# Low parts of the first layer's operands during attention: from DVE (five of seven) to POOL (all seven)

## The chip, the cores and the metric

One core of a Trainium2 chip runs the whole program. The metric is the device time of one launch in microseconds. The engines are TensorE (PE; its weight loads are listed as PEld), VectorE (DVE), ScalarE (ACT), GpSimd (POOL) and SyncE (SP, which only issues DMAs here). Each engine works through its own instructions in program order; between engines, semaphores keep the order of reads and writes.

## What is computed

An attention with a bias that a small network makes from positions, then two layers of experts that are all used, with their weights. Cut to what matters:

```python
# q, k, v: (2, 8, 576, 64)
scores = scale * q @ k.T + bias          # bias from |i - j|, through 32 hidden units
attn = softmax(scores)                   # by rows
x = (attn @ v)                           # -> (1152, 512)
# layer 1: 4 experts, given weights p        layer 2: 8 experts, weights P from a gate (Sinkhorn, 8 rounds)
for e in range(E):
    h = np.maximum(x @ w1[e], 0.0)       # 512 -> 1024
    out += p[:, e:e + 1] * (h @ w2[e])   # 1024 -> 512
```

## The kernel before

All matrix products of the expert layers are made from split numbers: an operand is written as a high part (a copy rounded to the matmul's format, made by ACT, L103) and a low part (the value less its high part, a subtraction, L104), and three products of parts are added. The first product of an expert (x @ w1) also uses a fast scheme with seven products in place of eight, so x is kept as seven operands: A11, A12, A22 are blocks of x, and S1 to S4 are sums and differences of blocks. `pieces(1, 0)` makes these operands for the first five token tiles ("chunk 0") of layer 1, out of the rows that attention has finished. Each tile of x10A and x10S in the profile is one of them.

The chunk has 5 pieces of 64 columns. A piece has three parts, and after the last there is one more flush:

- part1 first calls `flush()`, which issues the low parts that are pending from the part before. Then the engine `eng` makes t1 = a21 + a22 (L117), a21 = a11 - a21 in place (L118) and t2 = t1 - a11 (L119). Then `split` has ACT make the high parts of A12, A11 and S1 at once, and puts their low parts on the list of pending ones, in this order.
- part2 flushes (the low parts of A12, A11, S1), then `eng` makes a12 = a12 - t2 in place (L126); S2 and A22 are split.
- part3 flushes (S2, A22), then splits S3 (from a21) and S4 (from a12). Their low parts are issued by the flush of the next part1.

The parts are called with two engines, `eng` = DVE (`ve`) and `other` = POOL (`gp`): A11 and A22 have their low part made by `other`, the five others by `eng`.

They are worked off one by one in the attention's loop over the units k = 0 to 38. A unit is one pair of heads, one batch entry and one tile of 128 rows; there are 36. The order of work is written out by hand. In iteration k the engines get, in this order:

- DVE: emit_x(k-4) (L514: the output rows of unit k-4, from PSUM), then the scores of unit k are made on PE (L388), after the transposes (L443) of the tail of unit k-2, and its spread reciprocals, into the same PSUM tile. Then DVE's two maxima of unit k (L406, one for each head, which also write the scores to SBUF), then the reciprocal for unit k-1 (L429), after which POOL spreads it over 128 columns (L431).
- ACT: the first exponential of unit k (L419), the copy of the tail of unit k-2 (L488), its share of the copies of the transposed scores (L488), in the first half also two copies of the bias (L362), the second exponential of unit k. DVE makes the other copy (L486) or, while the bias is still being made, the hidden units (L319).
- POOL: L425 for unit k, which adds a small number to the two sums of the exponentials and so waits for the second exponential of unit k.
- PE: the product with V of unit k-3 (L504).
- DVE: the split of the queries for a later unit (L256, L257), in some iterations.
- one part of the pieces, in k = 16 to 18 and 23 to 35. So part1 stands in 16, 23, 26, 29 and 32, part2 in 17, 24, 27, 30 and 33, part3 in 18, 25, 28, 31 and 34, the last flush in 35.
- from k = 28, one step of the split of the first weights: POOL low parts of 128x512 (L170), with their high parts on ACT (L169), and differences on DVE (L166).

When the loop is over, the first layer begins (L751). The lines of the pieces and their calls:

Of the kernel before, what the change touches and what calls it, by code (L numbers as in the profile page):

```python
# [48 lines left out]
def attn_moe_moe(ctx: ExitStack, tc: tile.TileContext, pack, keep, rel, qT, kT, vT, w, out):  # L49
    nc = tc.nc  # L50
    pe, ve, sc, gp, sy = nc.tensor, nc.vector, nc.scalar, nc.gpsimd, nc.sync

    def pool(name, space=None, bufs=1, stack=ctx, side=None):
        kw = {} if space is None else {"space": space}
        if side is not None:
            kw["side"] = side
        if space is not DRAM:
            kw["reuse_waits"] = "tile"
        return stack.enter_context(tc.tile_pool(name=name, bufs=bufs, **kw))
# [25 lines left out]
    def col_tile(k):  # L85
        return row_tile(k).rearrange("p (k c) -> p k c", k=4)
# [4 lines left out]
    def pieces(layer, c):  # L91

        n = CHUNKS[c][1]
        for i in XA:
            X[layer, c, i] = xpools[c].tile([128, 2, 2, n], F32R, tag=f"x{c}{i}", name=f"x{layer}{c}{i}")


        pending = []

        def split(i, src, o, w, lo):  # L100
            x = X[layer, c, i]
            hi = x[:, 0, :, o:o + w]
            sc.activation(out=hi, in_=src, func=AF.Copy)  # L103
            pending.append(lambda: lo.tensor_tensor(out=x[:, 1, :, o:o + w], in0=src, in1=hi.bitcast(F32), op=ALU.subtract))  # L104

        def flush(eng=None, other=None):
            while pending:
                pending.pop(0)()

        def piece(k1, c1, k2, c2, w, o):  # L110
            h1, h2 = col_tile(k1)[:, :, c1:c1 + w], col_tile(k2)[:, :, c2:c2 + w]
            a11, a12, a21, a22 = h1[:, 0:2], h1[:, 2:4], h2[:, 0:2], h2[:, 2:4]
            t1, t2 = (g1.tile([128, 2, 128], F32, tag=f"t{i}", name=f"t{i}_{layer}{k1}")[:, :, 0:w] for i in range(2))

            def part1(eng, other):
                flush()
                eng.tensor_tensor(out=t1, in0=a21, in1=a22, op=ALU.add)  # L117
                eng.tensor_tensor(out=a21, in0=a11, in1=a21, op=ALU.subtract)  # L118
                eng.tensor_tensor(out=t2, in0=t1, in1=a11, op=ALU.subtract)  # L119
                split("A12", a12, o, w, eng)  # L120
                split("A11", a11, o, w, other)
                split("S1", t1, o, w, eng)

            def part2(eng, other):
                flush()
                eng.tensor_tensor(out=a12, in0=a12, in1=t2, op=ALU.subtract)  # L126
                split("S2", t2, o, w, eng)
                split("A22", a22, o, w, other)

            def part3(eng, other):  # L130
                flush()
                split("S3", a21, o, w, eng)
                split("S4", a12, o, w, eng)

            return [part1, part2, part3]

        return [part for x in CHUNKS[c][2] for part in piece(*x)] + [flush]
# [46 lines left out]
    def attention(moe):  # L184
# [232 lines left out]
        def emit_exp(u, h):  # L417
            s = sm[u][:, S * h:S * h + S]
            sc.activation(  # L419
                out=s, in_=s, func=AF.Exp, scale=-1.0,  # L420
                bias=stat[u][:, h:h + 1], accum_out=stat[u][:, 2 + h:3 + h],
            )
# [4 lines left out]
        def emit_recip2(u):  # L427
            st = stat.pop(u)
            ve.reciprocal(st[:, 6:8], st[:, 4:6])  # L429
            spread[u] = atb.tile([128, 128], F32, tag="spread", name=f"spread{u}", bufs=2)  # L430
            gp.tensor_copy(  # L431
                spread[u].rearrange("p (h d) -> p h d", h=2), st[:, 6:8].unsqueeze(2).to_broadcast([128, 2, D])
            )
# [78 lines left out]
        def emit_x(u):  # L512
            t, p, b = units[u]
            ve.tensor_tensor(  # L514
                out=rows[t][:, b, 128 * p:128 * p + 128],
                in0=po[t, p][:, 128 * b:128 * b + 128], in1=rc.pop(u), op=ALU.mult,
            )
# [6 lines left out]
        def busy(n):  # L524
            for _ in range(n):
                pe.matmul(out=po_all[:, 0, 0:128], lhsT=ones, rhs=ones, start=True, stop=True)  # L526
# [73 lines left out]
        ti, work, first_split = 0, [], None  # L600
        for k in range(U + 3):
            first = False
            if made == NGR and not apart:
                st_tq.close()
                tq, apart = pool("tr", PSUM, stack=st_tq, side="right"), True
            if k == FOUR:
                st_sc.close()
                ps, four = pool("ps4", PSUM, stack=st_sc, side="left"), True
            if k < U:
                t, p, b = units[k]  # L610
                first = b == 0
                if first:
                    ti = tps_.index((t, p))
                if k >= 4:
                    emit_x(k - 4)
                emit_S(k)
                if k < 3:
                    busy(6)
                emit_max(k)

                if (t == 4 or b == 1) and ti in follows:
                    wanted.append(follows[ti])
                while wanted and NEED[tps_[wanted[0]][0]] <= made:
                    load_bias(wanted.pop(0))
                if k > 0:
                    emit_recip2(k - 1)
                if first and ti + 4 < len(tps_):
                    load_q(*tps_[ti + 4])
                if k < 2:
                    load_k(*kq[k + 6])  # L630
                if k < 8 and k % 2 == 0:
                    load_v(k // 2)
            elif k == U:
                emit_recip2(k - 1)
                emit_x(k - 4)
                st_sc.close()
                st_a.close()
                moe.open1()
                first_layer = moe.L1(0)
                for fn in first_layer[0:3]:  # L640
                    fn()
            if k < U:
                emit_exp(k, 0)
                if k >= 2:
                    emit_evac(k - 2, 2, sc)
            if k >= 2 and k - 2 < U:
                emit_T(k - 2)
                one = made < NGR
                emit_evac(k - 2, 3 if one else 0, sc)
                if k >= U:  # L650
                    emit_evac(k - 2, 2, sc)
            if k < FOUR:
                emit_exp(k, 1)
            groups(1)
            if FOUR <= k < U:
                emit_exp(k, 1)
            if k >= 2 and k - 2 < U:
                if not one:
                    emit_evac(k - 2, 1, ve)
            hids(2)  # L660
            if k < U:
                emit_recip(k)
            hids(2)
            if k >= 3 and k - 3 < U:
                emit_P(k - 3)
                if k >= U:
                    emit_x(k - 3)

            if first:
                if ti + 2 < len(tps_) and tps_[ti + 2][0] < 4:  # L670
                    prep_q(*tps_[ti + 2])
            prep_lows()
            if k < 4:
                prep_k(*kq[k + 4], sc)
            if k == 8:
                gp.memset(wgr, 0.0)
                gp.tensor_copy(wgr[:, :, 0:E2], kept[:, K_WG:K_WG + 32].rearrange("p (k e) -> p k e", e=E2))
                ve.tensor_reduce(out=psm, in_=dp, axis=mybir.AxisListType.X, op=ALU.add)
                ve.tensor_scalar(psm, psm, 1e-9, None, op0=ALU.add)
                ve.reciprocal(psm, psm)  # L680
                ve.tensor_tensor(out=p1, in0=dp, in1=psm.unsqueeze(2).to_broadcast([128, NTT, E1]), op=ALU.mult)
            if k == 15:
                work = pieces(1, 0)
            if work and (15 < k < 19 or 22 < k):
                work.pop(0)(ve, gp)
            if k == 24:
                load_raw(0)
            if 28 <= k < U:
                if first_split is None:
                    first_split = moe.prefetch(-1, gp)  # L690
                if first_split:
                    first_split.pop(0)()
            if k == U:
                second_split = moe.prefetch(-1, ve)
                for fn in second_split[0:4] + first_layer[3:5]:
                    fn()
            if k == U + 1:
                for fn in first_layer[5:] + second_split[4:]:
                    fn()
# [409 lines left out]
```

## Time and profile before

| | us |
|---|---|
| median of the runs | 1336.52 (1336.31 to 1337.37) |
| profiled execution | 1338.04, of it a span of 1335.9 from the first to the last instruction |
| PE busy in the span | 1310.9 (98%) |
| DVE busy | 784.5 (59%) |
| ACT busy | 518.0 (39%) |
| POOL busy | 434.0 (32%) |

Shares of busy time are means over the attention (to about 171 us) and the two layers behind it, which have different limits. Times below are microseconds from the start of the span. In a timeline the time in square brackets is how long the engine was idle just before, and what ended that; a line without brackets began with no idle time worth a note. An instruction's duration includes its tail, which overlaps the next one of the same engine.

### The profile page before, as it was taken

What the parts mean: (1) busy time and instruction counts of PE and PEld (TensorE: products, weight loads), DVE (VectorE), ACT (ScalarE), POOL (GpSimd) and SP (SyncE); (2) the same over time, 40 slices, a digit from 0 to 9 for tenths busy, and PEclk for the clock granted to TensorE, in tenths of its full rate; (3) what the DMA queues carried; (4) which work ended last, traced back from release to release, by engine and by line L of the source; (5) the groups of instructions that cost most, each with busy time, mean ns of one, the idle gap of its engine ahead of it and who ended that gap; (6) DMA issues with size and microseconds to landing.
All of it is one profiled execution on the core that took longest, in us unless ns stands there. A gap on an engine that the chain in (4) does not pass through costs nothing.

```text
span 1335.9 us, 23119 instructions
## 1 busy us (share of the span) xinstructions
PE 1310.9 (98%) x9105; PEld 1147.5 (86%) x9105; DVE 784.5 (59%) x1766; ACT 518.0 (39%) x1208; POOL 434.0 (32%) x457
## 2 busy tenths in 40 slices
PE   7999899999999999999999999999999999999998
PEld 4777788898888898888888898998988988988987
DVE  7899967454553644864864644644735635645633
ACT  5899853441331422543342421422422413313311
POOL 5443432350440530450530620621612603504400
PEclk8999999999999999999999999999999999999999
DMA  7876421020110110020110210210201200201010
GB/s 228 225 221 165 136 66 43 32 95 0 64 65 0 64 64 1 32 96 1 64 64 1 65 62 1 95 32 1 95 32 33 95 0 33 95 1 63 33 40 32
DMA packets 34316, 84.71 MB, mean 63 GB/s; under 512 B 8864, under 2 KB 9120, under 8 KB 34208
## 3 DMA queue, kind: packets, MB, share of 16 engines
q1 hardware_dynamic: 31184, 75.60, 17.9%
q0 software_dynamic: 2880, 7.34, 2.0%
q8 instruction: 71, 1.16, 0.4%
q14 instruction: 37, 0.30, 0.1%
q10 hardware_dynamic: 144, 0.29, 0.1%
HBM read 69.97 MB, written 13.25 MB: 62 GB/s over the span
## 4 chain that ended last, share of the span: by engine, by line
PE 88%; DVE 5%; ACT 3%; DMA 2%; issue 1%; POOL 1%; SPq 0%; ACTq 0%; POOLq 0%; DVEq 0%
PE y L830 43%; PE B L751 16%; PE C L751 11%; PE A L751 11%; PE po L504 2%; PE sc L388 2%; PE bps L333 1%; DMA bd<-bsts 1%; DVE s L406 1%; ACT s L419 1%; ACT bsts L362 1%; DMA rawb<-in_w 1%; ACT at L488 1%; PE po L526 1%; PE tp L467 1%
## 5 line engine op out<-in xcount | busy, mean ns | idle before, releaser
L830 PE MATMUL y<-gb,h 128*128 128x512 f32 x2592 | 713.5, 395 | 0.0
L830 PEld LDWEIGHTS y<-gb,h 128*128 128x128 f32 x2592 | 450.7, 188 | 56.6 <-issue 0.4
L170 POOL TENSOR_TENSOR gb<-rawb,gb 128x512 fp32r<-128x512 f32 x94 | 122.9, 1322 | 630.3 <-ACT gb L169 625.8
L759 DVE TENSOR_TENSOR u<-B,s 128x320 f32<-128x320 f32 (+1 forms) x192 | 87.9, 458 | 334.7 <-PE B L751 334.7
L762 ACT ACTIVATE h<-c 128x320 fp32r<-128x320 f32 (+1 forms) x288 | 120.0, 439 | 366.3 <-DVE c L759 365.1
L765 DVE SCALAR_TENSOR_TENSOR h<-c,h 128x320 fp32r<-128x320 f32 (+1 forms) x288 | 180.1, 642 | 50.6 <-ACT h L762 45.6
L170 POOL TENSOR_TENSOR ga<-rawa,ga 128x512 fp32r<-128x512 f32 x94 | 127.6, 1376 | 3.3 <-ACT ga L169 3.2
L170 POOL TENSOR_TENSOR ga<-wt,ga 128x512 fp32r<-128x512 f32 x94 | 107.5, 1163 | 25.4 <-ACT ga L169 14.5
L759 DVE TENSOR_TENSOR c<-C,u 128x320 f32<-128x320 f32 (+1 forms) x192 | 87.2, 454 | 39.7 <-PE C L751 36.1
L773 ACT ACTIVATE s<-A 128x320 f32<-128x320 f32 (+1 forms) x96 | 39.5, 411 | 162.3 <-PE A L751 162.3
L169 ACT ACTIVATE gb<-rawb 128x512 fp32r<-128x512 f32 x96 | 60.0, 626 | 88.4 <-DMA rawb<-in_w 88.4
L762 ACT ACTIVATE h<-A 128x320 fp32r<-128x320 f32 (+1 forms) x96 | 39.0, 406 | 137.2 <-PE A L751 137.1
L759 DVE TENSOR_TENSOR c<-B,s 128x320 f32<-128x320 f32 (+1 forms) x96 | 43.9, 457 | 74.4 <-PE B L751 73.2
L751 PE MATMUL B<-x20S,ga 128*128 128x320 f32 x384 | 66.6, 309 | 0.0
L751 PE MATMUL C<-x20S,ga 128*128 128x320 f32 x384 | 66.6, 309 | 0.0
L751 PE MATMUL A<-x20A,ga 128*128 128x320 f32 x384 | 66.6, 309 | 0.0
L751 PEld LDWEIGHTS A<-x20A,ga 128*128 128x128 f32 x384 | 61.5, 188 | 5.7
L751 PEld LDWEIGHTS C<-x20S,ga 128*128 128x128 f32 x384 | 61.3, 188 | 5.7
L751 PEld LDWEIGHTS B<-x20S,ga 128*128 128x128 f32 x384 | 61.3, 188 | 5.6
L419 ACT ACTIVATE s<-s,stat 128x576 f32<-128x576 f32 x72 | 55.4, 770 | 11.3 <-DVE stat L406 9.6
L751 PEld LDWEIGHTS C<-x21S,ga 128*128 128x128 f32 x384 | 54.4, 188 | 6.3 <-DVE c L759 0.7
L751 PEld LDWEIGHTS A<-x21A,ga 128*128 128x128 f32 x384 | 54.5, 189 | 5.6
(194 smaller groups left out, 1880.7 us busy)
## 6 DMA issues: line engine op xcount, KB each, us to landing
rawa<-in_w SPq DMA_DIRECT2D x48, 512.0 KB, 4.0
rawb<-in_w SPq DMA_DIRECT2D x48, 512.0 KB, 4.9
bd<-bsts SPq DMA_DIRECT2D x36, 295.5 KB, 4.4
bt<-bd SPq DMA_DIRECT2D x13, 512.0 KB, 4.6
qr<-in_qT POOLq DMA_DIRECT2D x40, 64.0 KB, 3.7
kr<-in_kT POOLq DMA_DIRECT2D x16, 144.0 KB, 4.0
V<-in_vT POOLq DMA_DIRECT2D x4, 512.0 KB, 5.1
out<-rows SPq DMA_DIRECT2D x8, 256.0 KB, 2.1
```

The costliest lines, as they stand in the source:

```text
L169: sc.activation(out=z(0), in_=src, func=AF.Copy)
L170: lo.tensor_tensor(out=z(1), in0=src, in1=z(0).bitcast(F32), op=ALU.subtract)
L333: pe.matmul(out=o[32 * q:32 * q + 32, j, 0:n], lhsT=w2n, rhs=hid[g, q][:, n * j:n * j + n], start=True, stop=True,)
L388: pe.matmul(out=o[h][c:c + n, j, 0:288], lhsT=a[d, 128 * bb + c:128 * bb + c + n], rhs=m[d, 288 * j:288 * j + 288], start=t == 4 or i == 0 ...
L419: sc.activation(out=s, in_=s, func=AF.Exp, scale=-1.0, bias=stat[u][:, h:h + 1], accum_out=stat[u][:, 2 + h:3 + h],)
L504: pe.matmul(out=o[64 * h:64 * h + 64, c0:c0 + n], lhsT=V[p][:, j, col:col + D], rhs=rhs, start=j == 0, stop=j == 4,)
L751: pe.matmul(out=ban[o], lhsT=a, rhs=x[:, z, k, :], start=not more and i == 0, stop=i == 5, skip_group_check=more,)
L759: ve.tensor_tensor(out=t[o], in0=ban[a], in1=t[b], op=ALU.add)
L762: sc.activation(out=h[f][:, 0, half, :], in_=src, func=AF.Relu)
L765: ve.scalar_tensor_tensor(out=h[f][:, 1, half, :], in0=src, scalar=0.0, in1=h[f][:, 0, half, :].bitcast(F32), op0=ALU.max, op1=ALU.subtract,)
L773: sc.activation(out=t["s1"], in_=ban["A"], func=AF.Copy)
L830: pe.matmul(out=self.y[t], lhsT=a, rhs=x, start=g == 0 and f == 0 and i == 0, stop=g == NP - 1 and f == 1 and i == 2,)
```

## The change

The parts get a third engine, `low`, that makes the low parts which `eng` made; without it all is as before. The attention's loop now passes POOL for it, so in chunk 0 of layer 1 all seven low parts of each piece are POOL's. The sums and differences (L117, L118, L119, L126) stay on DVE. The other callers (chunk 1, layer 2) pass two engines and change nothing.

```diff
             def part1(eng, other, low=None):
                 flush()
+                low = low or eng
                 eng.tensor_tensor(out=t1, in0=a21, in1=a22, op=ALU.add)
                 eng.tensor_tensor(out=a21, in0=a11, in1=a21, op=ALU.subtract)
                 eng.tensor_tensor(out=t2, in0=t1, in1=a11, op=ALU.subtract)
-                split("A12", a12, o, w, eng)
+                split("A12", a12, o, w, low)
                 split("A11", a11, o, w, other)
-                split("S1", t1, o, w, eng)
+                split("S1", t1, o, w, low)

             def part2(eng, other, low=None):
                 flush()
                 eng.tensor_tensor(out=a12, in0=a12, in1=t2, op=ALU.subtract)
-                split("S2", t2, o, w, eng)
+                split("S2", t2, o, w, low or eng)
                 split("A22", a22, o, w, other)

             def part3(eng, other, low=None):
                 flush()
-                split("S3", a21, o, w, eng)
-                split("S4", a12, o, w, eng)
+                split("S3", a21, o, w, low or eng)
+                split("S4", a12, o, w, low or eng)
...
             if work and (15 < k < 19 or 22 < k):
-                work.pop(0)(ve, gp)
+                work.pop(0)(ve, gp, gp)
```

## Rows read from the trace of the kernel before

**Rows 1.** Busy time of PE, PEld, DVE, ACT, POOL; clock; DMA share; GB/s.

```profile
146.00:171.00 25.00, 20.77 (x357) 17.99 (x354) 22.49 (x76) 22.14 (x64) 13.30 (x25) 1.00 0.31 92
```

**Rows 2.** The chain in order of time, units 27 and 28: start, duration, what.

```profile
140.72 0.61 ACT s L419
141.59 0.28 ACT at L488
141.91 0.34 PE sc L443 x4
142.25 0.87 PE sc L388 x12
143.15 0.55 DVE s L406
144.03 0.61 ACT s L419
```

**Rows 3.** Timeline of DVE: start, duration, line, operation, out<-in, shapes [idle before].

```profile
104.57 0.28 DVE L126 TENSOR_TENSOR rows<-rows,t 128x128 f32<-128x128 f32 x1
104.97 0.74 DVE L406 CUSTOM_DVE_ANT_0 s<-sc,rows 128x576 f32<-128x576 f32 x1
...
131.86 0.76 DVE L406 CUSTOM_DVE_ANT_0 s<-sc,bt 128x576 f32<-128x576 f32 x1 [0.82 <-PE sc L388]
...
154.04 0.42 DVE L166 TENSOR_TENSOR wt<-rawa 128x256 f32<-128x256 f32 x1
...
154.58 0.75 DVE L406 CUSTOM_DVE_ANT_0 s<-sc,bt 128x576 f32<-128x576 f32 x1
...
165.07 0.76 DVE L406 CUSTOM_DVE_ANT_0 s<-sc,bt 128x576 f32<-128x576 f32 x1 [0.48 <-PE sc L388]
```

**Rows 4.** Line L104 by form: duration min/median/max in ns, first and last start.

```profile
L104 POOL TENSOR_TENSOR x10A<-rows,x10A x10: 453/458/464, 106.3 to 168.7; 128x128 fp32r<-128x128 f32 x10
...
L104 DVE TENSOR_TENSOR x10A<-rows,x10A x5: 280/281/349, 104.2 to 163.6; 128x128 fp32r<-128x128 f32 x5
```

**Rows 5.** Timeline of POOL in the five iterations with a part2.

```profile
105.99 0.21 POOL L425 TENSOR_SCALAR stat<-stat 128x2 f32<-128x2 f32 x1 [2.69 <-ACT s L419]
...
133.22 0.20 POOL L425 TENSOR_SCALAR stat<-stat 128x2 f32<-128x2 f32 x1 [1.79 <-ACT s L419]
133.50 0.45 POOL L104 TENSOR_TENSOR x10A<-rows,x10A 128x128 fp32r<-128x128 f32 x1
...
143.19 0.21 POOL L425 TENSOR_SCALAR stat<-stat 128x2 f32<-128x2 f32 x1 [1.41 <-ACT s L419]
...
154.09 0.44 POOL L425 TENSOR_SCALAR stat<-stat 128x2 f32<-128x2 f32 x1 [1.40 <-ACT s L419]
...
164.97 0.21 POOL L425 TENSOR_SCALAR stat<-stat 128x2 f32<-128x2 f32 x1 [1.12 <-ACT s L419]
```

**Rows 6.** Timeline of ACT: the first exponentials of units 18 and 25.

```profile
106.21 0.77 ACT L419 ACTIVATE s<-s,stat 128x576 f32<-128x576 f32 x1
...
133.42 0.77 ACT L419 ACTIVATE s<-s,stat 128x576 f32<-128x576 f32 x1
```

**Rows 7.** The chain in order of time: low parts on it, units 26 and 29.

```profile
138.60 0.40 DVE x10S L104 x2
...
148.56 0.56 DVE x10S L104 x2
```

**Rows 8.** Timeline of PE: transposes of the spread reciprocals that waited for POOL.

```profile
160.45 0.28 PE L443 MATMUL sc<-kept,spread 64*128 64x64 f32 x2 [0.23 <-POOL spread L431]
...
167.58 0.27 PE L443 MATMUL sc<-kept,spread 64*128 64x64 f32 x2 [0.16 <-POOL spread L431]
```

**Rows 9.** Layer 2: POOL and DVE timelines at 551 us; one form of L104.

```profile
551.43 0.98 POOL L104 TENSOR_TENSOR x20A<-rows,x20A 128x128 fp32r<-128x128 f32 x2
...
551.54 0.55 DVE L126 TENSOR_TENSOR rows<-rows,t 128x128 f32<-128x128 f32 x1
...
L104 DVE TENSOR_TENSOR x20S<-t,x20S x10: 279/284/1412, 534.1 to 553.1; 128x128 fp32r<-128x128 f32 x10
```

More of the change, by code (lines that the diff above doesn't have):

```diff
@@ L104, in split, with flush @@
             pending.append(lambda: lo.tensor_tensor(out=x[:, 1, :, o:o + w], in0=src, in1=hi.bitcast(F32), op=ALU.subtract))
-        def flush(eng=None, other=None):
+        def flush(eng=None, other=None, low=None):
             while pending:
@@ L113, in piece, with part1 @@
             t1, t2 = (g1.tile([128, 2, 128], F32, tag=f"t{i}", name=f"t{i}_{layer}{k1}")[:, :, 0:w] for i in range(2))
-            def part1(eng, other):
+            def part1(eng, other, low=None):
                 flush()
+                low = low or eng
                 eng.tensor_tensor(out=t1, in0=a21, in1=a22, op=ALU.add)
@@ L119, in part1, with part2, part3 @@
                 eng.tensor_tensor(out=t2, in0=t1, in1=a11, op=ALU.subtract)
-                split("A12", a12, o, w, eng)
+                split("A12", a12, o, w, low)
                 split("A11", a11, o, w, other)
-                split("S1", t1, o, w, eng)
-            def part2(eng, other):
+                split("S1", t1, o, w, low)
+            def part2(eng, other, low=None):
                 flush()
                 eng.tensor_tensor(out=a12, in0=a12, in1=t2, op=ALU.subtract)
-                split("S2", t2, o, w, eng)
+                split("S2", t2, o, w, low or eng)
                 split("A22", a22, o, w, other)
-            def part3(eng, other):
+            def part3(eng, other, low=None):
                 flush()
-                split("S3", a21, o, w, eng)
-                split("S4", a12, o, w, eng)
+                split("S3", a21, o, w, low or eng)
+                split("S4", a12, o, w, low or eng)
             return [part1, part2, part3]
```

## The prediction

> **What bounds the kernel now.** I read the busy times by stretch first, then the chain of work in order of time, then the timelines of DVE, POOL and ACT, iteration by iteration. TensorE is the busiest engine of the whole program, but the change sits in the second half of the attention, from about 100 to 171 us, and there it is not the bound: in the stretch from 146 to 171 us PE is busy 20.77 of 25 us, ACT 22.14, DVE 22.49, POOL only 13.30, at a granted clock of 1.00 [rows 1]. So POOL has room and DVE is nearly full, which is the case for the change. But shares say nothing of order. The chain does: one unit k of attention goes from the first exponential (L419) to the copy of the unit's tail (L488), to the tail's transposes on PE (L443), to the scores (L388), to the maximum on DVE (L406), and to the next first exponential, 140.72 to 144.03 [rows 2]. That loop of 3.31 us has no slack inside it; POOL is not in it. Whoever delays the maximum by a microsecond delays everything after it by a microsecond, until an iteration comes in which something else was late anyway.
>
> I number the units as the loop does (k = 0 to 35). The maxima of units 18, 25, 28, 31 and 34 start at 104.97, 131.86, 143.15, 154.58 and 165.07 [rows 2, 3].
>
> **What the change moves.** There are 5 pieces. Of each, 5 of 7 low parts go from DVE to POOL: 25 instructions of 128x128, 281 ns each on DVE, 458 ns on POOL by the 10 that POOL makes there already [rows 4]. The DVE instructions overlap their neighbours, so each frees about 0.2 us of DVE, 5 us in all. POOL issues them about 0.4 us apart, 10 us in all, which its idle time could hold. No DMA moves and no copy of ACT changes.
>
> **The wait that it adds.** The first instruction of part2 after the flush is the subtraction at L126, which overwrites a12 in place. The low part of A12 reads a12 and is the first thing in the flush just before. While both were DVE's, order on the engine was enough. Now L126 (DVE) must wait until POOL has made the low part of A12. POOL stands far behind DVE at this place of the program: ahead of the flush in its queue is L425 of the same unit, which waits for that unit's second exponential on ACT. In unit 17 DVE does L126 at 104.57 while POOL comes to L425 only at 105.99; the L425 of the other four part2s start at 133.22, 143.19, 154.09 and 164.97 [rows 3, 5]. Queued behind L126 on DVE are L514 and the next unit's maximum, which is in the loop of [rows 2]. L425 itself doesn't depend on anything that waits, so there is no deadlock, only a stall, once in each of the units 17, 24, 27, 30 and 33.
>
> Its size: from L425 to the low part that follows it is 0.28 (133.22 to 133.50), the low part is 0.46, and from L126 to the maximum is 0.40 when DVE runs through (104.57 to 104.97) [rows 3, 4, 5]. So the next maximum cannot start before L425 + 1.14. For the five:
> unit 17: 107.13 instead of 104.97, 2.16 late;
> unit 24: 134.36 instead of 131.86, 2.50 late;
> unit 27: 144.33 instead of 143.15, 1.18 late;
> unit 30: 154.09 + 1.14 + 0.34 for the L166 that stands between = 155.57 instead of 154.58, 0.99 late;
> unit 33: 166.11 instead of 165.07, 1.04 late.
> In the first two ACT was behind DVE, so part is absorbed: an exponential that waits only for its maximum starts 0.88 after it (143.15 to 144.03), hence at 108.01 instead of 106.21 and at 135.24 instead of 133.42 [rows 2, 6]. That leaves 1.80 and 1.82. In the last three the maximum was already awaited, nothing is absorbed. Sum 1.80 + 1.82 + 1.18 + 0.99 + 1.04 = 6.8 us. What is idle meanwhile does not catch up later: ACT's next work is the exponential that waits for the same maximum, and PE's next scores need the copy behind it.
>
> **What it gains.** In two iterations, 26 and 29, DVE runs without a gap from one maximum to the next and the two low parts of S3 and S4 lie on the chain: 0.40 and 0.56 us [rows 7]. They leave it: at most -0.96. The other low parts lie where DVE afterwards waits for PE, so they give nothing. The transposes of the spread reciprocals (L443) waited for POOL in two places. At 160.45 POOL's own queue was late, and with one more low part ahead it gets about 0.24 later (0.40 less the 0.16 that POOL idles there). At 167.58 it came 0.44 after the first transposes could go, and those are now 1.0 later themselves, so this wait goes, -0.4 [rows 8]. I take -1.0 for all of this, between -1.4 and 0.
>
> **The engines in each other's way.** L126 will start just as POOL begins the next low part of the same flush (A11). In layer 2 this meeting is in the trace: two low parts start on POOL at 551.43, L126 starts at 551.54 and takes 0.55 instead of 0.28 [rows 3, 9]. I add 0.27 for each of five, and as much for the L166 of unit 30, 1.6 us. The bounds: nothing, if L126 gets in first; and as large as the low part of 1412 ns against a median of 284 that stood behind a POOL instruction of 128x512 [rows 9], which only unit 30 can meet (the weights' low part follows there). The Trainium skill speaks against the change here: "SBUF — State Buffer", section "Who interferes with whom", says that a DVE instruction with two SBUF inputs contends with a POOL instruction that reads SBUF, and that who is first holds the port for the whole instruction. By that rule the price would be up to a whole low part of 0.46 each, 2.3 us for the five, and the forecast 0.7 us higher; the 0.27 of the trace agrees in kind, and I keep it.
>
> **The end of the attention.** The last flush (unit 35) now stands on POOL ahead of the last spread reciprocals, two low parts of 0.4 each; that spread lies about 0.7 ahead of its transposes, so 0 to 0.1. After 171 us nothing changes but the start.
>
> Sum: 6.8 - 1.0 + 1.6 = 7.4 us. The trace is of an execution of 1338.04 us (span 1335.9); the median is 1336.52, and I set the difference on that: 1343.9 us.
>
> **Rivals.** (a) Longer: the framework orders L118 too. Pieces 1 and 2, and 3 and 4, write columns of one tile beside each other; if the order is kept by extent and not by exact columns, the first DVE writes of units 26 and 32 wait for the low part of S3 behind L425, about 1.2 us each by the same working: 1346.3. The even interleaving of the two ranges speaks for it; nothing in the trace of before shows it either way, since no such pair crosses engines there. Chance 0.12.
> (b) Faster: DVE is the bound through this stretch, and the wait is covered. It needs POOL's low part of A12 to be done before DVE would come to L126 plus the slack, that is L425 at 0.74 before that point. Then the chain's 0.96 and the 0.4 count at least, and all 5 us that DVE is freed of at most: 1331.5 to 1335.1. For it: DVE's 22.49 of 25. Against it: in none of the five is L425 started when DVE does L126. It decides if DVE fell behind by 1.0 us or more anyway, which would need its queue to be the late one in all part2 iterations; in three of them it waited for PE before the maximum. A change that does not do what it says (low parts that come out in another order, A12 not first) would end in (b) only if A12 came ahead of L425, which the program order excludes. Chance 0.08.
> (c) No change: the stalls land, but in units 17 and 24 the rest of the stage (bias tiles, their transfers) was late by as much, and DVE's freed 5 us pays for the other three: 6.8 - 3.6 - 1.4 = 1.8 us or less, 1336.5 to 1338.3. For it speaks that both engines' queues are long there; against it that the chain of before goes through ACT and PE in these iterations and both wait for this maximum. Chance 0.08.
>
> **How the numbers follow.** The forecast has 0.72, its own bounds are 6.8 - 1.8 - 1.4 + 0 = 3.6 (half of the first two stalls absorbed, full gain, no contention) and 6.8 - 0 + 3.4 = 10.2 (0.46 at each, 1.1 more at unit 30): 1340.1 to 1346.7. With (a) mostly inside, the range is 1339.7 to 1347.2; it leaves out (b), (c) and some of (a). About 0.2% (2.7 us) is what a measurement here can tell from no change: slower 0.84 (the forecast and (a)), same 0.12 ((c) and the half of (b) above 1333.8), faster 0.04.
>
> **What would show it.** Right: in five places DVE idles before L126 and the releaser is POOL L104; POOL's L425 stands directly ahead of that low part; the maximum after it is 1 to 2.5 us later, and the loop's other iterations keep their lengths. The step on ports: L126 at about 0.55 instead of 0.28. Step "gains": units 26 and 29 shorter by 0.4 to 0.6. Wrong: no idle before L126; or idle before L118 as well (a); or idle before L126, but the first matmul of the first layer (L751) starts no later than now (c).

## The result and the profile after

The changed kernel takes 1346.81 us (median of 4, 1345.62 to 1347.81) against 1336.41 us (median of 4) for the kernel before: ratio 1.007, 95% interval 1.0059 to 1.0082. It is slower, by 10.4 us on the medians; the forecast was 1343.9, range 1339.7 to 1347.2. The profiled execution took 1345.62 us with a span of 1343.8, 7.9 more than the span before. Line numbers from L117 on are one higher than before: the subtraction that was L126 is L127, the maximum L406 is L407. In some experiments they shift further; each row has its own kernel's numbers.

The waits of the stage come first (timeline from 98 to 180 us; columns: who waited for whom, total us, times, longest):

```profile
...
ACT s L420 <- DVE stat L407: 12.4, 9, 2.0
DVE rows L127 <- POOL x10A L104: 11.4, 5, 3.5
...
PE po L505 <- DVE rows L515: 7.5, 5, 2.4
```

The second of these rows did not exist before: DVE stands idle five times, 11.4 us in all, until POOL has made a low part of x10A. The other two rows are its echo: ACT waits for the maximum behind it (3.9 us in 6 times before), PE for the output rows (L515) that stand between (0.9 us in 3 times before).

The timeline of DVE at the five places (these answer to [rows 3]):

```profile
106.01 0.53 DVE L127 TENSOR_TENSOR rows<-rows,t 128x128 f32<-128x128 f32 x1 [2.51 <-POOL x10A L104]
136.09 0.52 DVE L127 TENSOR_TENSOR rows<-rows,t 128x128 f32<-128x128 f32 x1 [3.49 <-POOL x10A L104]
147.72 0.53 DVE L127 TENSOR_TENSOR rows<-rows,t 128x128 f32<-128x128 f32 x1 [2.00 <-POOL x10A L104]
159.78 0.53 DVE L127 TENSOR_TENSOR rows<-rows,t 128x128 f32<-128x128 f32 x1 [1.34 <-POOL x10A L104]
172.77 0.53 DVE L127 TENSOR_TENSOR rows<-rows,t 128x128 f32<-128x128 f32 x1 [2.00 <-POOL x10A L104]
```

And POOL at the second of them (answers to [rows 5]):

```profile
135.33 0.21 POOL L426 TENSOR_SCALAR stat<-stat 128x2 f32<-128x2 f32 x1 [1.40 <-ACT s L420]
135.60 0.86 POOL L104 TENSOR_TENSOR x10A<-rows,x10A 128x128 fp32r<-128x128 f32 x2
136.43 0.50 POOL L104 TENSOR_TENSOR x10S<-t,x10S 128x128 fp32r<-128x128 f32 x1
```

L426 ends POOL's wait for the second exponential, the low parts of A12 and A11 follow, and DVE starts 0.49 after the first of them began. The chain in order of time around unit 27 shows that this is now the path (compare [rows 2], where POOL was not in it):

```profile
146.11 0.76 ACT s L420 x2
146.95 0.21 POOL stat L426
147.23 0.46 POOL x10A L104
147.78 0.38 issue
148.16 0.28 DVE rows L515
148.51 0.53 issue
149.23 0.61 ACT s L420
```

A stage is best measured by its landmarks. From the first maximum of unit 17 to the first matmul of the first layer (L751, L752 after; L754 to L763 in some experiments) it is 101.31 to 170.82 = 69.51 us before and 100.57 to 178.77 = 78.20 us after: +8.69. The span grew less, by 7.9, as the profiled run after reached unit 17 0.74 earlier; the traces of all kernels below reach it between 98.5 and 102.0, so the part ahead varies by more than that without any of the changes.

Split by the starts of the maxima, with the terms of the forecast beside them:

| units | before | after | difference | forecast |
|---|---|---|---|---|
| 17 to 24 (stall in 17) | 26.70 | 29.58 | +2.88 | 1.80 + 0.27 |
| 24 to 26 (stall in 24) | 7.82 | 9.85 | +2.03 | 1.82 + 0.27 |
| 26 to 27 | 4.02 | 3.61 | -0.41 | -0.40 |
| 27 to 28 (stall) | 3.30 | 4.76 | +1.46 | 1.18 + 0.27 |
| 29 to 30 | 4.31 | 4.03 | -0.28 | -0.56 at most |
| 30 to 31 (stall) | 3.82 | 5.35 | +1.53 | 0.99 + 0.54 |
| 31 to 32 | 3.29 | 4.08 | +0.79 | 0 |
| 32 to 33 | 3.75 | 3.54 | -0.21 | +0.24 |
| 33 to 34 (stall) | 3.45 | 4.77 | +1.32 | 1.04 + 0.27 |
| 34 to 35 | 3.68 | 3.28 | -0.40 | -0.4 |

The five stalls are as forecast. Three rows are not: 17 to 24 holds 0.8 more than its stall, 31 to 32 holds 0.79 that no part of the forecast explains, and 32 to 33 is shorter where it was forecast longer. PE's timeline at the first place:

```profile
106.79 1.31 PE L505 MATMUL po<-at,V 128*64 128x128 f32 x20 [1.42 <-DVE rows L515]
108.69 0.37 PE L444 MATMUL sc<-kept,s 64*128 64x64 f32 x2 [0.59 <-ACT at L489]
...
108.93 1.79 PE L389 MATMUL sc<-kk,qq 64*128 64x288 f32 x12
110.51 1.06 PE L468 MATMUL tp<-kept,s 64*128 64x64 f32 x16
...
113.95 1.04 PE L389 MATMUL sc<-kk,qq 64*128 64x288 f32 x12
```

The same twelve score matmuls (L389) take 1.79 us and, a unit later, 1.04. Below, those of 1.79 are called slow scores. Busy times by stretch (columns as in [rows 1]) tell why; the rows are of the changed kernel:

```profile
98.00:180.00 82.00, 67.69 (x1070) 55.14 (x1067) 62.59 (x194) 68.25 (x178) 39.14 (x90) 0.96 0.46 131
110.00:112.00 2.00, 2.00 (x26) 1.57 (x28) 1.78 (x5) 2.00 (x6) 0.67 (x3) 0.51 0.47 110
```

From 110 to 112 us the granted clock is 0.51: PE runs at the lower of its levels, 1.2 GHz, after it stood idle for 1.42 and 0.59 us with little work between. The kernel before has 1.00 in the stage [rows 1]. The second set of slow scores is at 163.28, behind the stall of unit 30, in the row 31 to 32.

### The profile page after: what moved, and what is told of

The parts are those of the page before. It is cut to its first block, busy times and chain, and to the rows that moved or that the text cites. A ratio compares the mean times of both kernels' runs of the same rounds, so it can differ in the third digit from the quotient of the medians.

```text
span 1343.8 us, 23142 instructions
## 1 busy us (share of the span) xinstructions
PE 1312.7 (98%) x9105; PEld 1149.0 (86%) x9105; DVE 776.7 (58%) x1741; ACT 517.5 (39%) x1208; POOL 443.2 (33%) x482
## 4 chain that ended last, share of the span: by engine, by line
PE 88%; DVE 5%; ACT 3%; DMA 2%; issue 1%; POOL 0%; SPq 0%; ACTq 0%; DVEq 0%; POOLq 0%
PE y L831 43%; PE B L752 17%; PE C L752 11%; PE A L752 11%; PE po L505 2%; PE sc L389 2%; PE bps L334 1%; ACT s L420 1%; DVE s L407 1%; DMA bd<-bsts 1%; ACT at L489 1%; PE tp L468 1%; ACT bsts L363 1%; DVE wt L167 1%; DVE rows L853 0%
## 5 line engine op out<-in xcount | busy, mean ns | idle before, releaser
L171 POOL TENSOR_TENSOR gb<-rawb,gb 128x512 fp32r<-128x512 f32 x94 | 122.9, 1322 | 628.8 <-ACT gb L170 621.6
L763 ACT ACTIVATE h<-c 128x320 fp32r<-128x320 f32 (+1 forms) x288 | 119.6, 439 | 365.7 <-DVE c L760 364.7
L766 DVE SCALAR_TENSOR_TENSOR h<-c,h 128x320 fp32r<-128x320 f32 (+1 forms) x288 | 176.7, 630 | 51.8 <-ACT h L763 46.8
L171 POOL TENSOR_TENSOR ga<-rawa,ga 128x512 fp32r<-128x512 f32 x94 | 128.0, 1381 | 2.7 <-ACT ga L170 2.7
L171 POOL TENSOR_TENSOR ga<-wt,ga 128x512 fp32r<-128x512 f32 x94 | 106.0, 1147 | 26.2 <-ACT ga L170 15.8
L763 ACT ACTIVATE h<-A 128x320 fp32r<-128x320 f32 (+1 forms) x96 | 38.8, 405 | 136.5 <-PE A L752 136.4
L752 PE MATMUL C<-x20S,ga 128*128 128x320 f32 x384 | 66.6, 309 | 0.0
L752 PE MATMUL A<-x20A,ga 128*128 128x320 f32 x384 | 66.6, 309 | 0.0
L752 PE MATMUL B<-x20S,ga 128*128 128x320 f32 x384 | 66.6, 309 | 0.0
L752 PEld LDWEIGHTS A<-x20A,ga 128*128 128x128 f32 x384 | 61.5, 188 | 5.7
L752 PEld LDWEIGHTS C<-x20S,ga 128*128 128x128 f32 x384 | 61.3, 188 | 5.7
L752 PEld LDWEIGHTS B<-x20S,ga 128*128 128x128 f32 x384 | 61.3, 188 | 5.6
L752 PEld LDWEIGHTS C<-x21S,ga 128*128 128x128 f32 x384 | 54.4, 188 | 6.3 <-DVE c L760 0.7
L505 PEld LDWEIGHTS po<-at,V 128*64 128x64 f32 x800 | 39.6, 138 | 23.4 <-DVE stat L407 11.3
```

The source lines that it names most:

```text
L171: lo.tensor_tensor(out=z(1), in0=src, in1=z(0).bitcast(F32), op=ALU.subtract)
L505: pe.matmul(out=o[64 * h:64 * h + 64, c0:c0 + n], lhsT=V[p][:, j, col:col + D], rhs=rhs, start=j == 0, stop=j == 4,)
L752: pe.matmul(out=ban[o], lhsT=a, rhs=x[:, z, k, :], start=not more and i == 0, stop=i == 5, skip_group_check=more,)
L763: sc.activation(out=h[f][:, 0, half, :], in_=src, func=AF.Relu)
L766: ve.scalar_tensor_tensor(out=h[f][:, 1, half, :], in0=src, scalar=0.0, in1=h[f][:, 0, half, :].bitcast(F32), op0=ALU.max, op1=ALU.subtract,)
```

## Experiments

The theory: the cost is one wait per piece. DVE's in-place subtraction of a12 waits for the low part of A12 on POOL, which stands in POOL's queue behind an instruction (L425, L426 after) that waits for ACT. The main rival: POOL gets 10 us more to do, its spread reciprocals come late, and it stands in DVE's way.

**e1: the low part of A12 back to DVE.** The other 20 stay on POOL.

```diff
-                split("A12", a12, o, w, low)
+                split("A12", a12, o, w, eng)
```

> The changed kernel, but the low part of A12 is DVE's again (5 of the 25 moved instructions go back), so the subtraction that overwrites a12 (L126 before, L127 after) waits for nobody. Theory (the cost is this one wait per piece, behind L425 on POOL): no idle time of DVE before the subtraction, the stage back to the length it had before, less up to 1 us for the low parts that leave the chain in units 26 and 29: 1335.5 to 1337.0 us. Rival (the cost is POOL's added 0.4 us for each low part, late spread reciprocals, and DVE and POOL in each other's way): 20 of 25 are still on POOL, so four fifths of 10 us stay: 1343 us or more.

Measured: 1336.50 us against 1337.37 of the kernel before in the same series, ratio 0.9994 (0.9984 to 1.0003). The stage takes 69.12 us (102.00 to 171.12), 0.39 less than before. The subtraction waits for nobody:

```profile
131.62 0.29 DVE L127 TENSOR_TENSOR rows<-rows,t 128x128 f32<-128x128 f32 x1
```

Five instructions of 25 carry the whole loss.

**e2: the low part of A12 alone on POOL.** The other 20 as before.

```diff
-                split("S1", t1, o, w, low)
+                split("S1", t1, o, w, eng)
...
-                split("S2", t2, o, w, low or eng)
+                split("S2", t2, o, w, eng)
...
-                split("S3", a21, o, w, low or eng)
-                split("S4", a12, o, w, low or eng)
+                split("S3", a21, o, w, eng)
+                split("S4", a12, o, w, eng)
```

> The kernel before, but the low part of A12 alone is POOL's (5 instructions moved instead of 25). Theory: the five stalls of 1.3 to 2.7 us stay whole, and the gain in units 26 and 29 (1 us) is not there, as S3 and S4 are DVE's: 1346.5 to 1348.5 us, with DVE idle before the subtraction five times, 10 to 12 us in all. Rival (the amount of work moved to POOL costs): a fifth of 10 us, about 1338.5 us.

Measured: 1347.53 us against 1337.37, ratio 1.0075 (1.006 to 1.009); the stage 79.60 us (99.65 to 179.25). The waits from 98 to 180 us:

```profile
DVE rows L127 <- POOL x10A L104: 10.4, 5, 3.5
```

So a fifth of the move gives at least as large a loss as the whole, and the rival in its plain form falls. The stage is even 1.40 us longer than with all 25 moved. Of this, 0.71 is the gain of units 26 and 29, which e2 doesn't have, and 0.80 stands in unit 30. There a low part of the weights (L171, 128x512) now follows on POOL at once, and the next instruction of DVE, L167, takes 1.48 us:

```profile
159.90 1.31 POOL L171 TENSOR_TENSOR gb<-rawb,gb 128x512 fp32r<-128x512 f32 x1
...
160.02 1.48 DVE L167 TENSOR_TENSOR wt<-rawa 128x256 f32<-128x256 f32 x1
```

In the changed kernel the low part of S1 (0.50 us) stands between the two on POOL, and the same L167 takes 0.67. The prediction had this as the upper bound of its port price in unit 30; the changed kernel did not meet it, e2 did.

**e3: all 25 on POOL, and a buffer of its own, n12, for a12 - t2.** Nothing overwrites a12 any more while POOL has to read it.

```diff
...
-                eng.tensor_tensor(out=a12, in0=a12, in1=t2, op=ALU.subtract)
+                eng.tensor_tensor(out=n12, in0=a12, in1=t2, op=ALU.subtract)
...
-                split("S4", a12, o, w, low or eng)
+                split("S4", n12, o, w, low or eng)
...
```

> The changed kernel with all 25 low parts on POOL, but a12 - t2 is written to a buffer of its own, from which S4 is made, so that nothing overwrites a12 while POOL still has to read it. Theory: no wait before the subtraction; 1335.5 to 1337.0 us; spread reciprocals may come up to 0.3 us later in two units. Rival (load of POOL, or the port): as slow as the changed kernel, 1345 us or more.

Measured: 1338.08 us against 1337.37, ratio 1.0008 (0.9998 to 1.0017); the time is 1 us above what I expected, and the stage has 70.34 us (98.77 to 169.11), 0.83 more than before. The wait is gone, but a smaller one has come in its place. The waits of this kernel, 98 to 180 us:

```profile
PE sc L449 <- POOL spread L437: 2.8, 6, 0.9
```

Before, PE waited for the spread reciprocals 3 times, 0.6 us in all; now 6 times and 2.8. Here the rival is right in kind: with all 25 low parts POOL's queue is late for the spread, and this is more than what units 26 and 29 gain. In the changed kernel the row reads 0.5 us, one time, because the stalls give POOL time to catch up. I had written up to 0.3 us later in two units, and that was too little.

**e4: all 25 on POOL, the flush ahead of L426.**

```diff
+            if work and (15 < k < 19 or 22 < k):
+                work[-1]()
             if k < U:
                 emit_recip(k)
```

> The changed kernel with all 25 low parts on POOL, but each flush is issued ahead of L425 of the same unit instead of behind it: on POOL the low parts then follow the spread of the reciprocals of the unit before, and wait for no exponential of this unit. Theory: the low part of A12 is done about 2.2 us after the unit's maximum starts, about when DVE comes to the subtraction (1.9 to 2.4 us after it), so a wait of 0 to 0.5 us stays, covered in three of five units by the wait for PE: 1335.5 to 1338.0 us. Rival (load of POOL, or the port): 1345 us or more.

Measured: 1337.79 us against 1337.37, ratio 1.0000 (0.9991 to 1.0009); the stage 69.96 us (98.50 to 168.46), 0.45 more than before. The wait for the low part of A12 shrinks from 11.4 us to

```profile
DVE rows L127 <- POOL x10A L104: 2.6, 3, 1.7
```

The same instructions on the same engines, only a place further forward in POOL's queue, are worth 8.24 us of the stage (78.20 less 69.96), the slow scores included, which e4 doesn't have. The wait of 1.7 us is in unit 24, where POOL was still issuing the DMAs of the queries; I had expected 0.5 at most.

**e5: as e2, but the low part of A11 on DVE,** so that POOL makes no further low part of the piece when the subtraction starts.

```diff
-                split("A11", a11, o, w, other)
+                split("A11", a11, o, w, eng if low is other else other)
```

> Like e2_only_a12_on_pool (only the low part of A12 moved), but the low part of A11 goes from POOL to DVE, so that POOL has nothing to do just when the subtraction L127 begins. Theory on the port (L127 takes 0.53 instead of 0.28 because POOL's next low part holds the shared read port): L127 takes 0.28 again, the stalls stay, each next maximum comes 0.25 earlier, 1.25 us in all: about 1346.3 us. Rival (the longer subtraction belongs to the wait itself): 0.53 stays, 1347.5 us as in e2.

Measured: 1345.93 us against 1337.17, ratio 1.0069 (1.0054 to 1.0084). The subtraction has its old length:

```profile
134.97 0.29 DVE L127 TENSOR_TENSOR rows<-rows,t 128x128 f32<-128x128 f32 x1 [3.33 <-POOL x10A L104]
```

From maximum to maximum the five stalls are 0.18, 0.23, 0.23, 0.23 and 0.25 us shorter than in e2, 1.12 in all. So the 0.25 us by which L127 is longer in the changed kernel come from POOL's next low part. The whole stage is 77.65 us, 1.95 shorter than in e2; most of the rest is one set of slow scores less (one in e5, two in e2). The Trainium skill ("SBUF — State Buffer", "Who interferes with whom") says that a DVE instruction with two SBUF inputs and a POOL instruction that reads SBUF contend; the trace agrees. The price is at most what was left of POOL's instruction when DVE started: in the changed kernel 0.25 us of 0.37 that were left at 106.01, in unit 30 of e2 1.06 of 1.19.

**e6 and e9: matmuls of ones in PE's idle time.** The changed kernel, with matmuls in the five stalls whose result is not used; `fill` issues them. e6 has 10, 18, 8, 13 and 6, e9 has 10, 9, 5, 7 and 3. Shown is their place for four of the stalls; for that of unit 17 (k = 18) they stand ahead of the bias matmuls.

```diff
...
+            if k in FILL and k > 18:
+                fill(k, pt.tile([128, 1, 512], F32, tag="bps", name=f"fill{k}", bufs=1))
             if k >= 3 and k - 3 < U:
                 emit_P(k - 3)
```

> The changed kernel with matmuls of ones (128x128, results not used) put into PE's queue just where PE stands idle in the stalls of units 17, 24, 27, 30 and 33: 10, 18, 8, 13 and 6 of them. Theory on the clock (PE's idle time in a stall is followed by scores at half the clock: 1.79 instead of 1.04 us, in two of five stalls of the profiled run, 0.7 to 0.8 us each): the granted clock stays at 1.00 through the stage, all scores take 1.04, the stalls of DVE stay as they are, and the time falls by 0.7 to 2 us: 1345 to 1346 us. Rival (slow scores have another cause): no change, 1346.8 us, scores of 1.79 still there. If the matmuls don't fit into the idle time, they cost instead up to 0.3 us each place.

> Like e6_pe_kept_busy, with fewer matmuls of ones, so that they end before PE's next own work is due: 10, 9, 5, 7 and 3. In e6 the clock stayed up, but its matmuls ran past the stall of unit 24 by 1.2 us and ate what they brought. Theory on the clock: clock 1.00, scores of 1.04 everywhere, and from the maximum of unit 17 to the first matmul of the first layer 78.20 less 0.75 and 0.4 to 0.8 for the two stretches of slow scores: 76.6 to 77.1 us. Rival (the stretches of slow scores cost nothing in the end): 78.2 us.

Measured: e6 1346.03 us against 1337.17, ratio 1.007 (1.0053 to 1.0086); e9 1346.16 against 1337.98, ratio 1.0067 (1.005 to 1.0084). The medians don't settle it, the traces do. In e6 all scores take 1.04 us; from the maximum of unit 18 to that of 20 it has 7.62 us instead of 8.38, from 31 to 33 7.20 instead of 7.62. But its 18 matmuls ran past the end of the stall in unit 24 and cost 1.22 us there, and the stage stayed at 78.51. e9 doesn't have that fault: the stage is 77.10 us (99.95 to 177.05), 1.10 less than in the changed kernel, at the upper end of what was expected. Against the kernel before that is 7.59 us more, and the forecast was 7.4. PE in e9 behind the stall of unit 17, and the stage by busy times:

```profile
103.84 2.50 PE L572 MATMUL bps<-ones 128*128 128x128 f32 x20 [0.18 <-ACT bsts L365]
...
108.50 1.04 PE L391 MATMUL sc<-kk,qq 64*128 64x288 f32 x12
```

```profile
98.00:180.00 82.00, 74.65 (x1140) 61.83 (x1139) 63.18 (x196) 67.87 (x178) 40.36 (x93) 1.00 0.45 129
```

**e10: the changed kernel again.**

> The changed kernel once more, on the same chip as e9. Theory: the stalls are of program order and come again with the same lengths, 2.4, 2.7, 1.5, 1.5 and 1.3 us from maximum to maximum beyond those of before; the slow scores need not come behind the same stalls, and their number changes the stretch from 78.2 by 0.4 to 0.8 each. Rival (the slow scores are bound to certain stalls, as the lengths of the idle times would have it): again behind units 17 and 30 and only there.

Measured: 1346.88 us against 1337.98, ratio 1.0072 (1.005 to 1.0095); the stage 78.38 us (99.76 to 178.14). The idle times before L127 are the same to 0.01 us (2.51, 3.49, 2.00, 1.34, 2.00). The slow scores are elsewhere:

```profile
137.45 1.78 PE L389 MATMUL sc<-kk,qq 64*128 64x288 f32 x12
...
149.85 1.79 PE L389 MATMUL sc<-kk,qq 64*128 64x288 f32 x12
```

They now follow the stalls of units 24 and 27; those of 17 and 30 go without. So the stalls are fixed by the program, and the clock falls behind some of them, not always the same. In e2 it fell behind the stalls of units 24 and 30, in e5 behind that of unit 30 alone, in e7 (one stall) not at all.

Unit 32 (32 to 33), whose predecessor has no slow scores here, is 3.98 long, 0.23 more than before: the transposes wait 0.46 for POOL's spread instead of the 0.23 of [rows 8].

```profile
166.86 0.28 PE L444 MATMUL sc<-kept,spread 64*128 64x64 f32 x2 [0.46 <-POOL spread L432]
```

In e9 it is 3.95.

**e7: only the first piece on POOL** (units 16 to 18).

```diff
-                work.pop(0)(ve, gp, gp)
+                work.pop(0)(ve, gp, gp if k < 19 else None)
```

> The changed kernel, but POOL makes all low parts of the first piece only (units 16 to 18); the four later pieces are as before. Theory: one stall is left, that of unit 17, worth 1.8 us after what ACT absorbs, 0.25 for the port, and 0.7 more if the clock falls: 2.0 to 2.8 us, 1338.5 to 1339.5 us, nothing regained in the units after. Rival (units 17 to 24 have slack from DVE's and ACT's long queues that absorbs a stall there): within 0.5 us of the kernel before.

Measured: 1339.14 us against 1337.17, ratio 1.0019 (1.0009 to 1.0028). The stage takes 71.62 us (99.68 to 171.30), 2.11 more than before; from the maximum of unit 17 to that of unit 24 it is 28.83 instead of 26.70. There are no slow scores in this trace, so 2.1 is the stall alone, and nothing of it is regained in seven units. The forecast had 1.80 + 0.27.

**e8: only S3 and S4 on POOL,** the low parts that lay on the chain.

```diff
-                split("A12", a12, o, w, low)
+                split("A12", a12, o, w, eng)
...
-                split("S1", t1, o, w, low)
+                split("S1", t1, o, w, eng)
...
-                split("S2", t2, o, w, low or eng)
+                split("S2", t2, o, w, eng)
```

> Only the low parts of S3 and S4 go to POOL (10 of 25); A12, S1 and S2 stay on DVE. These are the ones that lie on the chain in units 26 and 29. Theory: no stall, units 26 and 29 shorter by 0.4 and 0.3 to 0.5, no spread reciprocal later than before: 0.7 to 0.9 us faster, which the time can hardly show (0.05%) but the starts of the maxima can: the first matmul of the first layer 0.7 to 0.9 nearer to the maximum of unit 16 (74.07 us before). Rival (what leaves DVE comes back as a wait for PE or POOL at once): 74.07 again.

Measured: 1336.32 us against 1337.17, ratio 0.9997 (0.9987 to 1.0007): no difference that the time can show. The stage takes 68.46 us (99.62 to 168.08), 1.05 less than before: units 26 and 29 are 3.62 and 3.82 long instead of 4.02 and 4.31, and PE waits for the spread no more than before (0.5 us). Its stage is the shortest of all the versions, but by a single trace, and 1.05 us are less than a tenth of a percent of the time.

## Why the prediction was right, point by point

- **The wait that it adds:** shown. It is there five times, DVE for POOL's L104, with L426 directly ahead of it in POOL's queue. Taking away its cause in three ways (another engine for A12, another buffer, another place in the queue: e1, e3, e4) takes the loss away each time; putting A12 alone on POOL (e2) brings it.
- **Its size:** the forecast for the five stalls with their port price was 6.8 + 1.6 = 8.4 us; without the slow scores they measure 2.11 (from e7), 2.03, 1.46, 1.53 and 1.32, 8.45 in all. With the gains, e9, which has no slow scores, is 7.59 us above the kernel before; the forecast was 7.4. That ACT, being behind DVE, absorbs a part in units 17 and 24 and nothing in the others held too.
- **The port:** 0.25 each was measured, 0.27 was taken from one row of layer 2 [rows 9]. The second one for the L166 of unit 30 also came: it takes 0.67 at 160.23 (as L167) instead of 0.42. One sum of the prediction is off: the 0.7 us by which it has the rule's price higher compares five meetings at 0.46 with six at 0.27; five with five are 2.3 and 1.35, 0.95 apart. Neither the forecast nor its range used that 0.7.
- **The gain:** -0.41, -0.28 and -0.40 in units 26, 29 and 34; worked out were -0.40, at most -0.56, and -0.4. e8 has the gain of units 26 and 29 (-0.40, -0.49) without the loss. The +0.24 for unit 32 came out at -0.21 in the first trace of the changed kernel, whose unit 31 has slow scores and is 0.79 longer, so that POOL's spread was ready in time; without slow scores there it came, +0.20 in e9 and +0.23 in e10. And the reasoning that POOL's idle time "could hold" 10 us is right in the changed kernel only, where the stalls give POOL time; in e3, without stalls, PE waits 2.2 us more for the spread than before.
- **Rival (a), order by extent:** it fell. The first DVE writes of units 26 and 32 (L118, L119) don't wait; from 98 to 180 us DVE waits for POOL at L127 alone. (b) and (c) fell with the five waits and with e7.
- **What was missing:** the clock. I read 1.00 for every stretch before and did not ask what a stall does to it. In the profiled run it accounts for 1.1 to 1.6 of the 8.69 us (2.88 less 2.11 in the units behind the first stall and 0.79 in unit 31, some of it regained in unit 32; e9, with the clock held up, gains 1.10). The forecast has no term for it.
- **The range:** the change cost 10.4 us on the medians where 7.4 were forecast, and 1346.81 lies only 0.4 below the upper end of the range. The room above the forecast had been left for a dearer port and for rival (a). Neither came; the clock and the open rest below took it up. So the five stalls were right by their mechanism, and that the time stayed inside the range was in part luck.
- **Open:** the medians differ by 8.9 to 10.4 us, depending on the series, the stage by 8.7 and 8.9 in the two traces. Other executions than the traced ones may have slow scores behind more of the stalls; no trace shows it. The granted clocks of whole executions would fit: the four of e6 took 1344.24 and 1344.78 us at 0.999, 1347.28 and 1347.96 at 0.996, and the four of e10 went from 1344.43 us at 0.996 to 1350.29 at 0.991. Where in them the clock fell is not shown. That the part ahead of unit 17 varies by over 3 us between traces also stays unexplained.

## What to carry to other kernels

Work that is moved to an idle engine takes its place in that engine's queue with it: look at when the engine comes to that place, not at how busy it is. Here POOL was half idle, but it came to the flush 1 to 3 us later than DVE, behind an instruction that waits for ACT; an in-place update on DVE right behind the moved read turned that distance into a stall. Before moving a read, look for the next write to the same data: move the read that nobody overwrites (S3, S4), give the write its own buffer, or put the read further forward in the queue.

## What the runs showed of the hardware

- A stall on DVE can cost PE's clock. After 1.1 to 2.5 us of idle time before the product with V and 0.3 to 0.6 behind it, PE's granted clock fell to its lower level behind two of five stalls in each of the two traces of the changed kernel (0.51 from 110 to 112 us), behind two in e2 and one in e5, and twelve score matmuls took 1.79 instead of 1.04 us. Which stalls it hit differed between two executions of the same program; what decides that is open. The kernel before has idle times of up to 1.05 us of PE in this stage and a clock of 1.00. The Trainium skill ("TensorE: Matmul & The Clock Gate", "Part 1: The HAM clock gate (the "warmup" mystery)") says that PE's clock is halved when PE is idle; the 0.51 agrees with the level, and no run here shows when it falls. With matmuls of ones in the idle time the clock was 1.00 in the stage of e6 and of e9, and none of their ten stalls has slow scores behind it.
- A DVE subtraction with two SBUF inputs took 0.53 us instead of 0.28 when POOL had begun a subtraction of 0.46 us about 0.1 us before it (the changed kernel against e5). Behind a POOL subtraction of 1.31 us that had begun 0.12 us before, a DVE subtraction took 1.48 us instead of 0.42 (L167 in unit 30 of e2).
